# Batch 0's units in four quarter runs, and every second exact addition of weight words on GpSimd

## The chip, the cores and the metric

The kernel runs on one core of one Trainium2 chip. The time is the device time of one execution in microseconds; three runs of the kernel before gave 780.78 to 782.17, with a median of 781.16 us.

## The reference

Attention through packed queries feeds a two-layer network with a rational activation:

```
p_packed = softmax(p k^T / 8) v              # 8 batches, 8 heads, 576 keys, 32 packed rows, 64 wide
x        = softmax(q p_packed^T / 8) p_packed   # 576 queries a batch -> 4608 tokens x 512
h = x @ w_in                                 # 512 -> 2048
P = a0 + a1 h + a2 h^2 + a3 h^3
Q = 1 + |b0| |h| + |b1| h^2
out = (P / (Q + 1e-6)) @ w_out               # 2048 -> 512
```

q, k, v, p, a and the result are float32. The two weight matrices arrive as float64, so the kernel reads them as 64-bit words, 8 MB each, and turns them into float32 on the chip.

## The kernel before

**Tiling.** The tokens of a batch are split into two halves of 288, the 2048 features into eight chunks of 256. A *unit* (batch, half, chunk) is the work on 288 tokens and 256 features; there are 8 x 2 x 8 = 128, walked by u in the order batch, half, chunk. `hidden` (L876) makes h of a unit in PSUM, evaluates the rational function on ScalarE, VectorE and GpSimd (GpSimd adds U and U2; the quotient goes through a logarithm and an exponential on ScalarE), and leaves g in `gh`/`gl`. `acc_block` multiplies g by the rows of w_out and adds up over the eight chunks in two PSUM banks (ring `acc`, 128 tokens each, 256 of the 288); after the last chunk the sum is copied to SBUF and stored. The other 32 tokens of each half gather in `G` and are done for two batches at once in `remainder`.

x itself isn't formed: `m_chunk` multiplies the packed values by a chunk of w_in (tile `win`), so that h is this product (`M`) times the attention's weights (`AH`, `AL`). For batch 0 both are plain float32, for the later ones each operand is split into a high and a low part and three products are taken. The first 12 units (`PLAIN`) also multiply g by w_out undivided, in float32; from unit 12 on w_out is divided into two parts (`divide`, ScalarE and GpSimd), at the steps that `DIVIDE` lists.

**Words.** The weights come in 16 pieces of 1 MB: chunk c of w_in ("in") and of w_out ("out"). `words` sorts them by a due step: "in" c at c - 2, "out" c at c + 3 (`LAG`, as acc_block trails hidden by three units). `load_words` keeps up to five pieces ahead in buffers lent by the rings `m` and `w`; `room` says up to which piece each may be lent. `convert` turns one piece of 128 x 1024 words into float32: two ScalarE operations scale the upper and lower word, then VectorE masks the sign, shifts and joins, and adds the two as integers, exactly (shown in the profile as CUSTOM_DVE_ANT_0 with 2048 columns of 16 bits). The main loop converts one piece a step, and more where a due step asks for it; the first four are converted ahead of the loop.

**Order.** All operations of compute engines and DMAs are only recorded by these functions. `Planner` then sets each engine's order: it works out the data dependences (buffers' turns too), gives each operation a modelled cost, and schedules the list forward by ranks and backward to get new ranks, eight rounds, with 150 ns of slack added to each hand-over between engines on the way back. The best modelled end wins, and the engines' instructions are issued in that order (L288, so nearly all rows of the profile bear this line). In `schedule`, `shares` tells which operations the model keeps from overlapping between VectorE and GpSimd: all of GpSimd's, and of VectorE's the copies, operations with a scalar, and the integer addition, if no operand is in PSUM. Where the plan leaves PE idle in the first 150 us, matmuls with a tile of zeros (L285) are put in; they add nothing to the sums.

The attention of the next batch is spread through the loop's steps as filler (`fill`, `mt` for m_chunk); its first loads and the first words are pinned at the head of SP's queue. Batch 0's attention runs ahead of the first unit.

Of the kernel before, what the change touches and what calls it, by code (L numbers as in the profile page):

```python
# [31 lines left out]
class Planner:  # L32
# [24 lines left out]
    WAY.update({("sync", x): 80 for x in ENGINES})  # L57
    PASS = 200
    FIRST = {"tensor": 700.0, "vector": 800.0, "scalar": 2000.0, "gpsimd": 1400.0, "sync": 700.0}
    ROUNDS = 8  # L60
    SWITCH = 95
    SLACK = 150
    IN_FLIGHT = 8
    DMA_ISSUE, DMA_START, DMA_END = 420, 1400, 1200

# [70 lines left out]
    def shares(self, engine, calls):  # L136

        if engine == "gpsimd":
            return True
        if engine != "vector":  # L140
            return False
        name, args, _ = calls[0]
        aps = [x for x in args if isinstance(x, bass.AP)]
        if any(x.space == PSUM for x in aps):
            return False
        return name in ("tensor_scalar", "tensor_copy") or (name == "tensor_add" and aps[0].dtype == I32)

    def mode(self, engine, calls):

# [38 lines left out]
            edges.append(before)  # L188
        return edges

    def schedule(self, before, after, rank, back=False):

        n = len(rank)
        need = [len(x) for x in before]
        at, start, end = [0.0] * n, [0.0] * n, [0.0] * n
        soon = {e: [] for e in self.ENGINES}
        ready = {e: [] for e in self.ENGINES}
        free = dict.fromkeys(self.ENGINES, 0.0) if back else dict(self.FIRST)
        port = {"vector": 0.0, "gpsimd": 0.0}
        mode, landed, dma = None, [], 0.0  # L200
        for i in range(n):
            if not need[i]:
                heapq.heappush(soon[self.ops[i][0]], (0.0, rank[i], i))
        now = 0.0
        left = n
        while left:
            for e in self.ENGINES:
                while soon[e] and soon[e][0][0] <= now:
                    heapq.heappush(ready[e], heapq.heappop(soon[e])[1:])
                if free[e] > now or not ready[e]:  # L210
                    continue
                if e == "sync" and not back and len(landed) >= self.IN_FLIGHT and landed[-self.IN_FLIGHT] > now:
                    free[e] = landed[-self.IN_FLIGHT]
                    continue
                _, i = heapq.heappop(ready[e])
                left -= 1
                s = now
                if e == "tensor" and not back and self.modes[i] != mode:
                    s += self.SWITCH
                    mode = self.modes[i]  # L220
                if not back and self.shared[i]:
                    s = max(s, port["vector" if e == "gpsimd" else "gpsimd"])
                    port[e] = s + self.costs[i]
                start[i] = s
                end[i] = free[e] = s + self.costs[i]
                if e == "sync":
                    if back:
                        dma = max(dma, end[i]) + self.transfers[i]
                        end[i] = dma + self.DMA_START + self.DMA_END - self.DMA_ISSUE
                    else:  # L230
                        dma = max(dma, s + self.DMA_START) + self.transfers[i]
                        end[i] = dma + self.DMA_END
                        landed.append(end[i])
                for j in after[i]:
                    need[j] -= 1
                    f = self.ops[j][0]
                    way = self.WAY.get((f, e) if back else (e, f), self.PASS)
                    way += self.SLACK * (back and way > 0)
                    at[j] = max(at[j], end[i] + way)
                    if not need[j]:  # L240
                        heapq.heappush(soon[f], (at[j], rank[j], j))
            now = min(
                t
                for e in self.ENGINES
                for t in ([free[e]] if ready[e] else [max(soon[e][0][0], free[e])] if soon[e] else [1e12])
            )
        return start, end

    def order(self):
        n = len(self.ops)  # L250
        self.costs = [self.price(*x) for x in self.ops]
        self.transfers = [self.transfer(calls[0][1]) if engine == "sync" else 0 for engine, calls in self.ops]
        self.shared = [self.shares(*x) for x in self.ops]
        self.modes = [self.mode(*x) for x in self.ops]
        before = self.edges()
        after = [[] for _ in range(n)]
        for i, x in enumerate(before):
            for j in x:
                after[j].append(i)
        rank = list(range(n))  # L260
        best = None
        for r in range(self.ROUNDS):
            start, end = self.schedule(before, after, rank)
            if best is None or max(end) < best[0]:
                best = self.best = max(end), start, end
            s, e = self.schedule(after, before, [-x for x in end], True)
            m = max(e)
            rank = [m - x for x in e]
            rank[: self.pinned] = range(-self.pinned, 0)
        self.end, self.start = best[0], best[1]  # L270
        self.deps, self.t0 = dict(enumerate(before)), best[1]
        return sorted(range(n), key=lambda i: (best[1][i], i))
# [47 lines left out]
def attention_rational_ffn(  # L320
# [106 lines left out]


    words = [(kind, 2 * c, 2) for kind in ("in", "out") for c in range(NCH)]
    due = lambda x: x[1] // 2 + (LAG if x[0] == "out" else -2)  # L430
    words.sort(key=due)
    index = {(kind, i): r for r, (kind, j, n) in enumerate(words) for i in range(j, j + n)}

# [57 lines left out]
    def convert():  # L491
        nonlocal converted
        if converted == len(words):
            return
        load_words(AHEAD)
        (kind, i, n), raw = words[converted], words_in[converted][1]
        x = 4 if kind == "in" else n
        w = raw.bitcast(I32).rearrange("p (x y two) -> p x y two", x=x, two=2)
        lo, hi = w[:, :, :, 0], w[:, :, :, 1]

        if kind == "in":
            dst = win[:, i // 2]
            di = dst.bitcast(I32)
        else:
            dst = undivided(i // 2)
            di = dst.bitcast(I32)
        nc.scalar.activation(hi.bitcast(F32), hi.bitcast(F32), AF.Copy, scale=REBIAS)

        nc.scalar.activation(di, lo.bitcast(U32), AF.Copy, scale=2.0**-29)
        nc.vector.tensor_scalar(lo, hi, -0x80000000, None, ALU.bitwise_and)  # L510
        nc.vector.scalar_tensor_tensor(hi, hi, 3, lo, ALU.logical_shift_left, ALU.bitwise_or)
        nc.vector.tensor_add(dst.bitcast(I32), hi, di)
        converted += 1
        load_words(AHEAD)

# [358 lines left out]
    GS = {}  # L874

    def hidden(bb, x, c):  # L876
        plain = (2 * bb + x) * NCH + c < PLAIN
        mh, ml = (M[bb, c // 2][:, i, :, c % 2 * CF : (c % 2 + 1) * CF] for i in range(2))
        parts = [(mh, AH[bb])] if bb == 0 else [(mh, AH[bb]), (ml, AH[bb]), (mh, AL[bb])]
        U, V, Y = U_ring.next(), V_ring.next()[:, :, 0:HALF], Y_ring.next()  # L880
# [1 line left out]
        for f in range(2):  # L882
            h = h_ring.next()[:, 0:HALF]
            for i, (w, a) in enumerate(parts):
                for g in range(NG):
# [1 line left out]
                        h, w[:, g, f * P : (f + 1) * P], a[:, g, x * HALF : (x + 1) * HALF],  # L887
                        start=g == 0 and i == 0, stop=g == NG - 1 and i == len(parts) - 1,
                    )
            u, y = U[:, f, :], Y[:, f, :]  # L890
            nc.scalar.activation(y, h, AF.Identity, scale=reg_a3, bias=a2)
            nc.scalar.activation(u, h, AF.Abs, scale=reg_b0)
            nc.scalar.activation(U2[:, f, :], h, AF.Square, scale=reg_root)
            nc.vector.tensor_mul(y, y, h)
            nc.vector.scalar_tensor_tensor(y, y, a1, h, ALU.add, ALU.mult)
# [8 lines left out]
        yield  # L904
        r0 = (bb % 2) * REM + x * HREM
        if plain:
            g = GS[bb, x, c] = (gh_ring if c % 2 == 0 else gl_ring).at(c // 2 % 2, dtype=F32)
            for o, cols in ((g, slice(0, HMAIN)), (G[:, 2 * c : 2 * c + 2, r0 : r0 + HREM], slice(HMAIN, HALF))):
                nc.vector.scalar_tensor_tensor(
                    o, V[:, :, cols], 2.0, Y[:, :, cols], ALU.subtract, ALU.mult, reverse0=True  # L910
# [37 lines left out]


    units = [(bb, x, c) for bb in range(B) for x in range(2) for c in range(NCH)]  # L950
    NU = len(units)
    UB = 2 * NCH
    ACC, O = {}, {}

    def acc_block(u, i):
        bb, x, c = units[u]
        if c == 0 and i == 0:
            ACC[bb, x] = [acc_ring.next() for _ in range(2)]
        acc = ACC[bb, x][i]
        cols = slice(i * P, (i + 1) * P)  # L960
        if u < PLAIN:
            for f in range(2):
                g = GS[bb, x, c][:, f, cols]
                nc.tensor.matmul(acc, g, X[c][:, f, :], start=c == 0 and f == 0, stop=c == NCH - 1 and f == 1)
        else:
            gh, gl = GS[bb, x, c]
        for f in range(0 if u < PLAIN else 2):
            accumulate(acc, gh[:, f, cols], gl[:, f, cols], 2 * c + f, c == 0 and f == 0, c == NCH - 1 and f == 1)
        if c < NCH - 1:
            return  # L970
        if i == 0:
            O[bb, x] = o_next()
# [2 lines left out]
        ov = out[bb * T : bb * T + NS * P, :].rearrange(order, i=2, x=2)[:, x]  # L975
        if u == NU - 1 and i == 1:
            nc.vector.tensor_copy(o[:, i, :], acc)
        else:
            nc.scalar.copy(o[:, i, :], acc)
        if u == NU - 1:  # L980
# [20 lines left out]
    STEPS = 16  # L1001
    mt, fill, rem = {}, {}, {}
    for c in range(1, NCH):
        mt[max(0, 2 * c - 3)] = 0, c
    for bb in range(1, B):
        for c in range(0, NCH, 2):
            mt[2 * UB * bb + 2 * c - 7] = bb, c, 2
# [95 lines left out]
```

## Time and profile before

| | |
|---|---|
| median of three runs | 781.16 us (780.78 to 782.17) |
| profiled execution | 780.48 us, span 778.7 us |
| PE / DVE / ACT / POOL busy | 743.9 / 690.6 / 654.8 / 451.8 us |
| mean granted TensorE clock | 0.99 |
| read from and written to HBM | 45.62 MB, 9.44 MB |

Engines: PE is the matmul engine, PEld its weight load, DVE VectorE, ACT ScalarE, POOL GpSimd, SP the queue that issues all DMAs. Times in the views count from the start of the span. A float32 matmul leaves two records. Names such as `w<-w` are output and input tiles with buffer numbers left out; as the words lie in buffers of the rings `m` and `w`, the operations of a conversion show as `m<-m`, `w<-w`, `win<-m,win`, `win<-w,win`, `w<-w,w` or `half<-w,half`.

### The profile page before, as it was taken

The numbers are of one execution on the slowest core, as the hardware profiler recorded it, in microseconds if no ns is written. First come the engines' busy times: TensorE is split into PE (matmuls) and PEld (weight loads), VectorE is DVE, ScalarE is ACT, GpSimd is POOL, SyncE is SP. The second block draws the span as 40 slices with busy tenths as digits, with TensorE's granted clock in tenths as the row PEclk, the third lists the DMA queues.
The fourth block names the chain that finished last, engine by engine and source line by source line (L and its number), as shares of the span: only waits on it lengthen the run. The fifth ranks groups of instructions, "written<-read, shape, count | busy, mean of one in ns | idle before, by whom it ended". The sixth has DMA issues, their size and how long they took to land.

```text
span 778.7 us, 15003 instructions
## 1 busy us (share of the span) xinstructions
PE 743.9 (96%) x5350; PEld 569.8 (73%) x5350; DVE 690.6 (89%) x1295; ACT 654.8 (84%) x1464; POOL 451.8 (58%) x448
## 2 busy tenths in 40 slices
PE   2769999999999999999999999999999999999997
PEld 2435554678788787778788787778778787778886
DVE  4899999987998879998998889998999789998872
ACT  5889978998887988998897898998898798898881
POOL 0012357756695556765596556855586556856663
PEclk9979999999999999999999999999999999999999
DMA  9984260023601155022701128021801023000001
GB/s 299 369 272 145 103 122 28 1 86 53 105 1 55 45 60 98 1 86 38 120 1 55 45 38 120 1 64 41 112 27 55 34 46 40 14 12 17 28 0 42
DMA packets 152028, 56.04 MB, mean 72 GB/s; under 512 B 122256, under 2 KB 141200, under 8 KB 151952
## 3 DMA queue, kind: packets, MB, share of 16 engines
q1 hardware_dynamic: 151952, 55.07, 30.3%
q8 instruction: 42, 0.69, 0.4%
q14 instruction: 34, 0.28, 0.1%
HBM read 45.62 MB, written 9.44 MB: 71 GB/s over the span
## 4 chain that ended last, share of the span: by engine, by line
PE 71%; DVE 12%; ACT 11%; DMA 2%; issue 2%; POOL 1%; SPq 0%; DVEq 0%; ACTq 0%; POOLq 0%
PE acc L288 37%; PE h L288 22%; PE at L288 12%; DVE Y L288 4%; DVE w L288 2%; ACT V L288 2%; ACT Y L288 2%; DVE small L288 2%; DVE kx L288 2%; DMA nat<-in_k_dram 2%; ACT U L288 2%; ACT sq L288 1%; ACT half L288 1%; ACT w L288 1%; DVE V L288 1%
## 5 line engine op out<-in xcount | busy, mean ns | idle before, releaser
L288 POOL TENSOR_TENSOR U<-U,sq 128x576 f32<-128x576 f32 x128 | 184.9, 1444 | 102.1 <-ACT U L288 47.5
L288 PE MATMUL acc<-w,gh 128*128 128x512 f32 x736 | 236.9, 406 | 0.3
L288 PE MATMUL h<-AH,m 128*128 128x288 f32 x1024 | 200.6, 318 | 4.7 <-DVE Y L288 4.0
L288 PEld LDWEIGHTS h<-AH,m 128*128 128x128 f32 x1024 | 160.0, 189 | 45.8 <-DVE Y L288 24.5
L288 POOL TENSOR_TENSOR gl<-Y,gh 128x512 fp32r<-128x512 f32 x116 | 150.4, 1296 | 46.1 <-ACT gh L288 15.2
L288 PEld LDWEIGHTS acc<-w,gh 128*128 128x128 f32 x736 | 133.5, 188 | 44.0 <-issue 9.0
L288 ACT ACTIVATE Y<-h,abS 128x288 f32<-128x288 f32 x256 | 128.5, 518 | 25.0 <-PE h L288 20.1
L288 PE MATMUL acc<-w,gl 128*128 128x512 f32 x384 | 148.1, 412 | 0.2 <-DVE w L288 0.2
L288 ACT ACTIVATE sq<-h 128x288 f32<-128x288 f32 x256 | 108.9, 428 | 34.9 <-PE h L288 26.7
L288 DVE TENSOR_TENSOR Y<-Y,h 128x288 f32<-128x288 f32 x256 | 109.0, 444 | 26.7 <-ACT sq L288 11.6
L288 DVE SCALAR_TENSOR_TENSOR Y<-Y,abS,V 128x576 f32<-128x576 f32 x128 | 102.9, 804 | 27.5 <-ACT V L288 26.7
L288 DVE SCALAR_TENSOR_TENSOR Y<-Y,abS,h 128x288 f32<-128x288 f32 x256 | 124.7, 505 | 2.2
L288 ACT ACTIVATE U<-h 128x288 f32<-128x288 f32 x256 | 102.5, 432 | 11.2 <-DVE V L288 7.4
L288 ACT ACTIVATE V<-U,one 128x576 f32<-128x576 f32 x128 | 99.4, 777 | 10.8 <-DVE Y L288 7.9
L288 PE MATMUL h<-AL,m 128*128 128x288 f32 x448 | 96.0, 295 | 0.0
L288 DVE SCALAR_TENSOR_TENSOR V<-U,V 128x576 f32<-128x576 f32 x128 | 95.8, 749 | 0.0
L288 DVE SCALAR_TENSOR_TENSOR Y<-V,Y 128x576 f32<-128x576 f32 x116 | 86.3, 744 | 1.4
L288 PEld LDWEIGHTS acc<-w,gl 128*128 128x128 f32 x384 | 71.3, 188 | 20.1 <-issue 6.4
L288 ACT ACTIVATE V<-V 128x576 f32<-128x576 f32 x128 | 85.5, 668 | 0.4
L288 PE MATMUL acc<-half,gh 128*128 128x512 f32 x240 | 78.7, 409 | 0.0
L288 ACT CAST gh<-Y 128x512 fp32r<-128x512 f32 x116 | 73.7, 635 | 2.0 <-DVE Y L288 1.3
L288 PEld LDWEIGHTS h<-AL,m 128*128 128x128 f32 x448 | 71.8, 188 | 0.6 <-issue 0.5
(135 smaller groups left out, 955.5 us busy)
## 6 DMA issues: line engine op xcount, KB each, us to landing
w<-in_moe_w_out_dram SPq DMA_DIRECT2D x16, 512.0 KB, 4.4
out_dram<-half SPq DMA_DIRECT2D x15, 512.0 KB, 3.1
nat<-in_k_dram SPq DMA_DIRECT2D x48, 144.0 KB, 3.8
nat<-in_q_dram SPq DMA_DIRECT2D x48, 144.0 KB, 4.3
nat<-in_v_dram SPq DMA_DIRECT2D x24, 256.0 KB, 3.3
m<-in_moe_w_in_dram SPq DMA_DIRECT2D x8, 512.0 KB, 5.7
w<-in_moe_w_in_dram SPq DMA_DIRECT2D x8, 512.0 KB, 9.6
nat<-in_k_dram SPq DMA_DIRECT2D x4, 512.0 KB, 8.5
```

Source lines behind the costliest of these rows:

```text
L288: getattr(getattr(self.nc, engine), name)(*args, **kwargs)
```

## The change

The first 16 units, those of batch 0, run in another order: half 0 with chunks 0 to 3, half 1 with 0 to 3, half 1 with 4 to 7, half 0 with 4 to 7. So a unit's place is no longer its formula but is looked up in `units`; the due steps of words and of m_chunk follow: chunks 4 to 7 of "in" are due at steps 6 to 9 instead of 2 to 5, those of "out" at 11 to 14 instead of 7 to 10. The order of the pieces was in0 to in5, out0, in6, out1, in7, out2, out3, out4 to out7; it becomes in0 to in3, out0, out1, out2, in4, out3, in5, in6, in7, out4 to out7.

Half 0 is now summed in two runs. Its first sum leaves PSUM after chunk 3 (a ScalarE copy into a buffer of the ring AL, which batch 0 doesn't use), and at the end VectorE adds it to the second, where ScalarE copied before.

The exact addition of every second piece (odd in the order of conversion) is issued on GpSimd. The planner's `shares` now counts every VectorE operation with two operands of more than eight columns and none in PSUM, and it tries five values of slack with six rounds each.

```
-    ROUNDS = 8
+    ROUNDS = 6
     SWITCH = 95
-    SLACK = 150
+    SLACK = 60, 100, 150, 220, 300
...
-        return name in ("tensor_scalar", "tensor_copy") or (name == "tensor_add" and aps[0].dtype == I32)
+        wide = sum(self.columns(x) > 8 for x in aps[1:])
+        return wide > 1 or name in ("tensor_scalar", "tensor_copy")
...
-                    way += self.SLACK * (back and way > 0)
+                    way += back * (way > 0)
...
-        rank = list(range(n))
+        first = self.schedule(before, after, list(range(n)))
         best = None
...
+        for slack in self.SLACK:
+            start, end = first
+            for r in range(self.ROUNDS):
+                s, e = self.schedule(after, before, [-x for x in end], slack)
+                m = max(e)
+                rank = [m - x for x in e]
+                rank[: self.pinned] = range(-self.pinned, 0)
+                start, end = self.schedule(before, after, rank)
+                if best is None or max(end) < best[0]:
+                    best = self.best = max(end), start, end
...
-    due = lambda x: x[1] // 2 + (LAG if x[0] == "out" else -2)
+    first = lambda c: c if c < NCH // 2 else c + NCH // 2
+    due = lambda x: first(x[1] // 2) + (LAG if x[0] == "out" else -2)
...
-        nc.vector.tensor_add(dst.bitcast(I32), hi, di)
+        (nc.gpsimd if converted % 2 else nc.vector).tensor_add(dst.bitcast(I32), hi, di)
...
-        plain = (2 * bb + x) * NCH + c < PLAIN
+        u = units.index((bb, x, c))
+        plain = u < PLAIN
...
-            g = GS[bb, x, c] = (gh_ring if c % 2 == 0 else gl_ring).at(c // 2 % 2, dtype=F32)
+            g = GS[bb, x, c] = (gh_ring if u % 2 == 0 else gl_ring).at(u // 2 % 2, dtype=F32)
...
+    cut = NCH // 2
+    units[:2 * NCH] = [(0, x, y * cut + c) for x, y in ((0, 0), (1, 0), (1, 1), (0, 1)) for c in range(cut)]
...
-        if c == 0 and i == 0:
+        fresh, whole = c in ((0, cut) if (bb, x) == (0, 0) else (0,)), c in ((cut - 1, NCH - 1) if (bb, x) == (0, 0) else (NCH - 1,))
+        if fresh and i == 0:
             ACC[bb, x] = [acc_ring.next() for _ in range(2)]
...
+        if not whole:
+            return
         if c < NCH - 1:
+            if i == 0:
+                O[0] = AL_ring.at(0, dtype=F32)
+            nc.scalar.copy(O[0][:, i, 0:DM], acc)
             return
...
+        elif (bb, x) == (0, 0):
+            nc.vector.tensor_add(o[:, i, :], acc, O[0][:, i, 0:DM])
         else:
             nc.scalar.copy(o[:, i, :], acc)
...
-        mt[max(0, 2 * c - 3)] = 0, c
+        mt[max(0, 2 * first(c) - 3)] = 0, c
```

More of the change, by code (lines that the diff above doesn't have):

```diff
@@ L189, in edges, with schedule @@
         return edges
-    def schedule(self, before, after, rank, back=False):
+    def schedule(self, before, after, rank, back=0):
         n = len(rank)
@@ L259, in order @@
                 after[j].append(i)
-        rank = list(range(n))
+        first = self.schedule(before, after, list(range(n)))
         best = None
[L262 to L269, printed above, removed]
+        for slack in self.SLACK:
[8 more added lines that the diff above has]
+                    best = self.best = max(end), start, end
         self.end, self.start = best[0], best[1]
@@ L889, in hidden @@
                     )
-            u, y = U[:, f, :], Y[:, f, :]
+            uf, y = U[:, f, :], Y[:, f, :]
             nc.scalar.activation(y, h, AF.Identity, scale=reg_a3, bias=a2)
-            nc.scalar.activation(u, h, AF.Abs, scale=reg_b0)
+            nc.scalar.activation(uf, h, AF.Abs, scale=reg_b0)
             nc.scalar.activation(U2[:, f, :], h, AF.Square, scale=reg_root)
@@ L963, in acc_block @@
                 g = GS[bb, x, c][:, f, cols]
-                nc.tensor.matmul(acc, g, X[c][:, f, :], start=c == 0 and f == 0, stop=c == NCH - 1 and f == 1)
+                nc.tensor.matmul(acc, g, X[c][:, f, :], start=fresh and f == 0, stop=whole and f == 1)
         else:
@@ L967, in acc_block @@
         for f in range(0 if u < PLAIN else 2):
-            accumulate(acc, gh[:, f, cols], gl[:, f, cols], 2 * c + f, c == 0 and f == 0, c == NCH - 1 and f == 1)
+            accumulate(acc, gh[:, f, cols], gl[:, f, cols], 2 * c + f, fresh and f == 0, whole and f == 1)
+        if not whole:
+            return
         if c < NCH - 1:
+            if i == 0:
+                O[0] = AL_ring.at(0, dtype=F32)
+            nc.scalar.copy(O[0][:, i, 0:DM], acc)
             return
```

## Prediction

> **What bounds the kernel now.** I read the page's first lines, then the busy time by stretches, the chain that ended last, the timeline of the first 140 us, the groups by shape. The page says where time is left.
>
> ```profile
> PE 743.9 (96%) x5350; PEld 569.8 (73%) x5350; DVE 690.6 (89%) x1295; ACT 654.8 (84%) x1464; POOL 451.8 (58%) x448
> PE   2769999999999999999999999999999999999997
> ```
>
> PE is busy nearly everywhere but in the first three of 40 slices (58 us) and the last. The busy time by stretches (columns: PE, PE's weight load, DVE, ACT and POOL, then the granted clock, DMA share and rate) cuts it finer.
>
> ```profile
> 20.00:30.00 10.00, 7.47 (x140) 6.10 (x126) 7.22 (x19) 8.10 (x18) 0.00 (x0) 0.83 1.08 360
> 30.00:46.30 16.30, 9.89 (x101) 4.95 (x99) 16.15 (x39) 12.90 (x24) 0.00 (x0) 0.79 1.05 358
> 46.30:60.00 13.70, 10.89 (x61) 6.00 (x62) 12.83 (x20) 12.92 (x28) 3.11 (x3) 0.87 0.75 245
> 60.00:92.00 32.00, 31.91 (x217) 18.14 (x216) 31.54 (x59) 30.56 (x69) 11.02 (x8) 1.00 0.39 135
> 92.00:139.00 47.00, 46.26 (x279) 24.73 (x280) 46.97 (x90) 39.63 (x81) 29.72 (x22) 1.00 0.31 63
> 110.00:150.00 40.00, 39.26 (x196) 18.87 (x195) 39.10 (x77) 35.50 (x75) 32.97 (x27) 1.00 0.15 29
> ...
> 150.00:303.60 153.60, 153.30 (x1167) 123.89 (x1165) 135.86 (x257) 129.43 (x302) 94.44 (x97) 1.00 0.32 59
> 303.60:481.04 177.44, 176.25 (x1329) 140.57 (x1329) 161.81 (x308) 152.91 (x352) 112.92 (x115) 1.00 0.29 55
> 481.04:658.50 177.46, 175.52 (x1328) 140.57 (x1328) 163.25 (x311) 153.45 (x352) 113.33 (x115) 1.00 0.26 49
> 658.50:778.70 120.20, 115.86 (x640) 94.89 (x640) 95.22 (x171) 92.94 (x210) 75.59 (x76) 0.99 0.06 21
> ```
>
> From 30 to 139 us DVE has no time left (16.15 of 16.30, then 12.83 of 13.70, 31.54 of 32.00, 46.97 of 47.00): 107.5 busy of 109. PE is idle 2.53, 6.41, 2.81, 0.09 and 0.74 us in the five stretches from 20 to 139. From 150 us on PE is the bound: 0.30, 1.19 and 1.94 us idle in the next three.
>
> PE's busy time between 60 and 92 us isn't all work. Line 285 issues matmuls against a tile of zeros where the planner expects PE to wait:
>
> ```profile
> L285 PE MATMUL acc<-half,zero 128*64 128x96 f32 x20 | 2.3, 254 | 0.0
> L285 PE MATMUL acc<-w,zero 128*64 128x96 f32 x18 | 2.1, 254 | 0.0
> ```
>
> These 38 records (columns: busy time, mean ns of one, idle before) are 2.3 + 2.1 = 4.4 us. So PE loses some 8 us between the first hidden matmul and 139 us (2.81 + 4.4 + 0.09 + 0.74), with DVE full beside it, and before that waits on the chain of batch 0's attention, which goes through DVE too. Pieces of that chain (start, length, what):
>
> ```profile
> 27.86 0.10 DVE win L288
> 27.96 0.95 issue
> 28.91 0.34 DVE small L288
> ...
> 39.74 1.08 DVE w L288
> ...
> 44.39 1.14 DVE w L288
> ...
> 46.27 0.82 PE h L288 x2
> ```
>
> Word conversions (the pieces that write win and w) stand in the attention's way: DVE runs whatever comes next in its order, and the attention's small operation of 28.91 us waited for an addition that writes win.
>
> **The change part by part.** The prices, from the groups by shape (first 130 us, then whole run):
>
> ```profile
> L288 DVE SCALAR_TENSOR_TENSOR w<-w 128x1024 int32<-128x1024 int32 x12 | 15.4, 1286 | 0.0
> L288 DVE TENSOR_SCALAR w<-w 128x1024 int32<-128x1024 int32 x12 | 9.0, 753 | 0.0
> L288 DVE CUSTOM_DVE_ANT_0 w<-w,w 128x2048 uint16<-128x2048 uint16 x6 | 7.6, 1262 | 0.0
> ...
> L288 POOL TENSOR_TENSOR U<-U,sq 128x576 f32<-128x576 f32 x128 | 184.9, 1444 | 102.1 <-ACT U L288 47.5
> L288 POOL TENSOR_TENSOR gl<-Y,gh 128x512 fp32r<-128x512 f32 x116 | 150.4, 1296 | 46.1 <-ACT gh L288 15.2
> L288 DVE TENSOR_TENSOR full<-at,full 128x512 f32<-128x512 f32 x12 | 8.2, 686 | 9.0 <-PE at L288 9.0
> L288 ACT COPY half<-acc 128x512 f32<-128x512 f32 x31 | 18.2, 603 | 12.6 <-PE acc L288 6.8 <-PE at L288 5.8
> ```
>
> One conversion on DVE is 0.75 + 1.29 + 1.26 = 3.30 us, the last term the exact addition.
>
> *Additions on GpSimd.* Eight of the 16 conversions lose the 1.26 us on DVE. By the new order of the words these are in1, in3, out1, in4, in5, in7, out5 and out7. The first four conversions begin before 30 us; so two of the eight (in1, in3) lie there, in1's beside idle DVE (worth nothing), in3's at 27.86, in the chain (0.10 + 0.95: 1.05 us). The other six take 6 x 1.26 = 7.6 us out of the full stretch. No integer addition on GpSimd is in this trace. Its nearest rows are float additions of 512 and 576 columns, 1296 and 1444 ns: 148 ns for 64 columns is 2.31 ns a column, and 1024 columns give 1444 + 448 x 2.31 = 2480 ns, my value. Bounds: 1444 ns (as for the shorter row) and twice the value, 4960 ns, if integers or the stride of two words cost as much again. GpSimd is busy 3.11 of 13.70 us and 11.02 of 32.00 us in the stretches up to 92 us. So four of the six lie beside idle GpSimd at no cost to it; out5 and out7 are due at the end, where GpSimd is busy 32.97 of 40 us; 2 x 2.48 fits in the 7.03 left, 2 x 4.96 does not. Behind an addition on GpSimd stand the U additions, for which ACT's logarithm waits.
>
> *What an addition on GpSimd does to DVE.* The timeline shows both engines at once, in one place with operands in SBUF on both sides and in one with an operand of DVE's in PSUM:
>
> ```profile
> 74.78 1.22 DVE L288 CUSTOM_DVE_ANT_0 half<-w,half 128x2048 uint16<-128x2048 uint16 x1
> 75.26 2.01 POOL L288 TENSOR_TENSOR U<-U,sq 128x576 f32<-128x576 f32 x1 [4.74 <-ACT sq L288]
> 76.28 1.56 DVE L288 TENSOR_SCALAR w<-w 128x1024 int32<-128x1024 int32 x1
> ...
> 55.93 1.42 POOL L288 TENSOR_TENSOR U<-U,sq 128x576 f32<-128x576 f32 x1 [5.14 <-ACT sq L288]
> ...
> 56.51 0.75 DVE L288 SCALAR_TENSOR_TENSOR V<-U,V 128x576 f32<-128x576 f32 x1
> ```
>
> In the first, POOL's addition took 2.01 us for 1.42 and DVE's next conversion step 1.56 us for 0.75: they waited for each other. In the second, with V in PSUM, neither is longer. All loop operations of a plain unit on DVE read PSUM, so only conversion steps can be held. I take 0.3 us of DVE a moved addition (between nothing and 0.81, the wait just seen), 6 x 0.3 = 1.8 us; the full addition, 2.48 us, is the upper bound and a rival below. The Trainium skill, SBUF — State Buffer, section "Who interferes with whom", with the section on the two sides ahead of it, has the port pair of the two engines locked for a whole instruction, against DVE operations with two SBUF inputs too. The trace agrees at 75.26 us: 1.42 us after the 1.22 us addition ended at 76.00, at about 77.3 us, POOL is done. This rule speaks against the change, and its worst case is that rival.
>
> *The order of units and words.* Batch 0 now runs chunks 0 to 3 for both halves of the tokens, then 4 to 7. By the due steps, 14 conversions are due by step 8 before and 11 after: 3 x 3.30 = 9.9 us of DVE less ahead of unit 8, which begins here:
>
> ```profile
> 99.51 0.65 PE L288 MATMUL h<-AH,m 128*128 128x288 f32 x2
> ```
>
> They come later, where DVE is also full (46.97 of 47.00), so the order alone removes no DVE work. It moves need from where PE waits (46 to 92 us) to where PE has work queued. The same holds for ACT's two steps a conversion, and for half of the m_chunk copies. The loads of words go the same way: SP issues out0 to out2 ahead of in4; the attention's own loads keep their places, and a word's buffer that GpSimd now releases some 1.2 us later has others of its ring free.
>
> *The sums kept half-way.* The first half's accumulators go to SBUF after chunk 3: two more copies on ACT, 2 x 0.60 us, hidden by ACT's idle (39.63 of 47.00). The end of that half is two DVE additions from PSUM in place of two ACT copies: 2 x 0.69 = 1.4 us more on DVE. The accumulators change hands three times, not two; PE has hidden matmuls in between, so I take 0.2 us, up to 1.2 if it waits for both copies. Plain units stay the first 12, so the matmuls are the same in number and kind.
>
> *The planner.* Five spreads of slack with six rounds each can pick another order for all 128 units. PE's idle in the steady stretches is 0.30, 1.19 and 1.94 us, so it can win 1 to 3 us at most there; I take zero.
>
> *Sum.* DVE's account: -7.6 + 1.8 + 1.4 = -4.4 us of the full stretch, and -1.05 ahead of it: -5.5. PE's account gives what can be used: 1.05 of chain, half of the 2.81 idle (the rest is the latency of the first units), most of the 4.4 of zeros, less 0.2: 1.05 + 1.4 + 3.5 - 0.2 = 5.8 us. Both must hold; I take -5.5. Against the profiled execution, 780.48 us with a span of 778.7, that is 775.0; it lies 0.68 under the median of 781.16, so the forecast is 775.6 us.
>
> **The rivals.** Each is counted from the median, 781.16.
>
> *Given back in the second half:* the conversions moved to units 8 to 12 and the two late additions meet a full DVE and a POOL of 32.97 in 40 us; PE then waits there for in5 to in7 and out4. For it: those two rows. Against: DVE can convert ahead, the words' buffers allow five. Half of the 9.9 us comes back as waiting: 5.5 - 4.9 = 0.6 gained, 780.6.
>
> *The additions hold DVE (the slower side):* place, DVE's conversion steps from 30 to 130 us; price 2.48 us for each of six, 14.9 + 1.4 - 7.6 = +8.7 us, and with the 1.05 of chain gained +7.6, 788.8; it decides from a mean of (7.6 + 1.05 - 1.4) / 6 = 1.2 us of waiting a moved addition. For it: the pair at 75.26. Against: conversion steps are 12 x 3.30 = 39.6 of the 107.5 us, and the rest of DVE's time isn't held. At 1.6 us a wait it is 9.6 + 1.4 - 8.65 = +2.4, 783.5.
>
> *A worse plan for the later batches:* same code from 150 us on in another order; at another 1.94 us in each of the three stretches, -5.5 + 5.8, 781.5. Against: the order before keeps PE at 99% with the same model.
>
> *More than I count:* all of the 2.81 + 4.4 + 0.83 and the 1.05 of chain, with two more of the conversion pieces in the chain (1.08 + 1.14), -11.3: 769.9. Against: DVE's account doesn't pay for it unless less waits on order.
>
> *The change doesn't do what it says:* the integer addition at 4.96 us makes POOL the bound at 110 to 150 us: 2 x 4.96 - 7.03 = 2.9 lost of the 5.5, 778.6.
>
> **How the numbers follow.** Forecast (772 to 778.5) 0.55; given back 0.12; held 0.13; worse plan 0.06; more 0.08; slow integer addition 0.06. The range of eight in ten goes from 769 (the "more" case) to 783, which takes in the cases near zero and leaves out most of "held". A difference under 0.2%, 1.6 us, can't be told from none. Faster: forecast, more, slow addition, and part of given back and worse plan, 0.77. Same: the rest of these two, 0.10. Slower: held, 0.13.
>
> **What would show it.** Right: fewer than ten zero matmuls; the hidden matmul of 46.27 us at 45.3 or before; GpSimd additions of 1024 columns near 2.5 us; DVE's conversion steps at 1.3 and 0.75 us still; PE's idle from 46 to 139 under 2 us; the last unit of batch 0 some 5 us earlier, and the same difference at the end. Wrong: conversion steps on DVE longer by 1 us or more; PE waiting for win or w between 95 and 130 us; idle of more than 2 us in a steady stretch of two batches.

## The result and the profile after

The changed kernel took 776.39 us (median of four, 775.34 to 777.33) against 780.97 us (four runs, 780.40 to 782.17): a ratio of 0.9939 with an interval of 0.9927 to 0.9951, 4.6 us faster. A second measurement, beside the last experiments, gave 776.94 against 782.43 us, 0.9927 (0.9910 to 0.9945).

The profiled execution took 777.33 us, 3.15 less than the one before (780.48). The first lines of the page after, and the busy time by the same stretches as in the prediction:

```profile
PE 738.7 (95%) x5332; PEld 567.8 (73%) x5332; DVE 687.9 (89%) x1289; ACT 653.3 (84%) x1464; POOL 473.0 (61%) x456
PE   1679999999999999999999999999999999999997
```

```profile
20.00:30.00 10.00, 6.60 (x154) 4.75 (x153) 7.98 (x19) 8.36 (x18) 2.42 (x1) 1.00 1.04 345
30.00:46.30 16.30, 11.61 (x106) 6.00 (x105) 15.32 (x37) 11.15 (x22) 1.32 (x2) 0.71 1.04 335
46.30:60.00 13.70, 10.21 (x77) 6.37 (x77) 12.89 (x21) 13.70 (x31) 7.01 (x4) 0.97 1.07 360
60.00:92.00 32.00, 31.34 (x221) 17.59 (x220) 32.00 (x63) 31.98 (x68) 15.02 (x10) 1.00 0.44 144
92.00:139.00 47.00, 46.98 (x264) 23.73 (x263) 45.85 (x83) 39.50 (x83) 35.42 (x24) 1.00 0.21 27
110.00:150.00 40.00, 39.74 (x211) 20.98 (x211) 39.50 (x77) 33.44 (x73) 33.06 (x27) 1.00 0.09 27
```

DVE is still full from 46 to 92 us, and PE is idle 3.49, 0.66 and 0.02 us from 46 to 139 (2.81, 0.09 and 0.74 before). DVE's busy time fell by 2.7 us over the run (690.6 to 687.9), where eight additions of 1.23 us left it and two of 0.69 came. POOL rose by 21 us. The groups by shape say where it went:

```profile
L291 POOL TENSOR_TENSOR w<-w,w 128x1024 int32<-128x1024 int32 x3 | 8.2, 2747 | 2.0 <-DVE w L291 2.0
L291 POOL TENSOR_TENSOR win<-m,win 128x1024 int32<-128x1024 int32 x3 | 7.3, 2417 | 9.9 <-DVE small L291 7.7 <-DVE m L291 2.2
L291 POOL TENSOR_TENSOR win<-w,win 128x1024 int32<-128x1024 int32 x2 | 4.8, 2414 | 6.2 <-DVE w L291 6.2
L291 DVE SCALAR_TENSOR_TENSOR w<-w 128x1024 int32<-128x1024 int32 x11 | 15.0, 1367 | 0.0
L291 DVE TENSOR_SCALAR w<-w 128x1024 int32<-128x1024 int32 x11 | 9.5, 873 | 0.2 <-ACT w L291 0.2
L291 DVE TENSOR_SCALAR m<-m 128x1024 int32<-128x1024 int32 x5 | 4.8, 962 | 9.9 <-ACT win L291 8.4 <-DMA AH<-in_q_dram 1.6
```

A GpSimd addition takes 2.41 us when nothing is in its way. The steps that stayed on VectorE became longer. All of VectorE's rows for the 16 conversions add up to 51.8 us before (masks 11.8, joins 20.3, additions 19.7) and to 46.1 us after (14.3, 21.1, 10.7): 5.7 us less, not 9.0 (what the additions alone fell by, 19.7 to 10.7), because masks and joins grew by 3.3 us, 2.5 of it in the masks. And it isn't conversions alone that wait. The timeline after, in batch 0's attention:

```profile
25.30 2.42 POOL L291 TENSOR_TENSOR win<-m,win 128x1024 int32<-128x1024 int32 x1 [7.74 <-DVE small L291]
...
25.77 1.98 DVE L291 TENSOR_TENSOR small<-small 128x4 f32<-128x4 f32 x1 [0.33 <-ACT small L291]
...
45.27 2.41 POOL L291 TENSOR_TENSOR w<-w,w 128x1024 int32<-128x1024 int32 x1 [2.04 <-DVE w L291]
...
45.74 2.50 DVE L291 TENSOR_SCALAR w<-w 128x1024 int32<-128x1024 int32 x1
```

An operation on four columns, 0.16 us by itself, took 1.98: it ended at 27.75, just behind GpSimd's addition (27.72). The mask of 45.74 us, 0.69 by itself, ended at 48.24, 0.56 behind the end of the addition (47.68). A mask has only one operand in SBUF beside its constant (`lo = hi & 0x80000000`), so it isn't operations with two SBUF operands alone that are held.

### The profile page after: what moved, and what is told of

Read it like the earlier page. It is cut to its first block, busy times and chain, and to the rows that moved or that the text cites. A ratio compares the mean times of both kernels' runs of the same rounds, so it can differ in the third digit from the quotient of the medians.

```text
span 775.5 us, 14985 instructions
## 1 busy us (share of the span) xinstructions
PE 738.7 (95%) x5332; PEld 567.8 (73%) x5332; DVE 687.9 (89%) x1289; ACT 653.3 (84%) x1464; POOL 473.0 (61%) x456
## 4 chain that ended last, share of the span: by engine, by line
PE 68%; DVE 16%; ACT 6%; DMA 5%; issue 2%; POOL 2%; SPq 1%; DVEq 0%; ACTq 0%
PE acc L291 35%; PE h L291 20%; PE at L291 12%; DVE Y L291 7%; DMA m<-in_moe_w_in_dram 2%; DVE V L291 2%; DVE kx L291 2%; DVE m L291 2%; DVE small L291 2%; DMA w<-in_q_dram 1%; ACT Y L291 1%; DMA w<-in_moe_w_in_dram 1%; DMA w<-in_moe_w_out_dram 1%; ACT sq L291 1%; ACT V L291 1%
## 5 line engine op out<-in xcount | busy, mean ns | idle before, releaser
L291 DVE TENSOR_TENSOR Y<-Y,h 128x288 f32<-128x288 f32 x256 | 111.2, 449 | 20.7 <-ACT U L291 7.7
L291 POOL COPY G<-Y 128x64 f32<-128x64 f32 x116 | 27.5, 237 | 76.5 <-DVE Y L291 68.1
```

What stands on the lines that cost most here:

```text
L291: getattr(getattr(self.nc, engine), name)(*args, **kwargs)
```

## The experiments

Each run is timed beside the kernel before on the same chip (782.4 to 782.7 us there).

**The change's three parts, each alone and in pairs.** Parts: the *order* (units, words, the sum kept half-way), the *additions* on GpSimd, the *planner* (five slacks, new sharing rule). With both kernels these are all eight combinations.

Order alone: the changed kernel with the class Planner of before, and with this line as before:

```
-        (nc.gpsimd if converted % 2 else nc.vector).tensor_add(dst.bitcast(I32), hi, di)
+        nc.vector.tensor_add(dst.bitcast(I32), hi, di)
```

> Batch 0's new order (units, words, the sum kept half-way) alone; all exact additions on VectorE and the planner as before. Theory (DVE's account, as in the prediction): the order removes no DVE work and adds two additions of 0.69 us, so with DVE full from 30 to 139 us it gives between +1 and -2 us against the kernel before, 779 to 782. Rival 1 (the order is what pays, because PE waits early and not late): -3 to -5, 776 to 778. Rival 2 (the planner's wider search is what pays): 0.

Additions alone, on the kernel before:

```
-        nc.vector.tensor_add(dst.bitcast(I32), hi, di)
+        (nc.gpsimd if converted % 2 else nc.vector).tensor_add(dst.bitcast(I32), hi, di)
```

> Every second exact addition on GpSimd alone; order of units and words and the planner as before. Theory: -8 x 1.26 us of DVE less some locking, -3 to -5 us, 776 to 778. Rival 1 (the additions hold DVE about as long as they free it; the trace after has 5.8 us less DVE saved than the eight additions are long): between +1 and -1. Rival 2: 0.

Planner alone, the changed class (with its loop over the slacks) in the kernel before:

```
+    SLACK = 60, 100, 150, 220, 300
...
+        wide = sum(self.columns(x) > 8 for x in aps[1:])
+        return wide > 1 or name in ("tensor_scalar", "tensor_copy")
```

> The planner alone (five slacks of six rounds, the new rule of what shares the port); all else as before. Theory: within 1 us of the kernel before, as PE is idle only 3.4 us in the three steady stretches. Rival 2 (the search is what pays): -3 to -5 us, 776 to 778.

Order and planner, the changed kernel with `nc.vector.tensor_add` for all pieces:

> The changed kernel with all exact additions on VectorE again. Theory: loses most of the gain, 779 to 781 (the changed kernel has 776.4). Rival 1 (the additions don't pay, the order does): 775 to 777.5, as the changed kernel or better.

Order and additions, the changed kernel with the class Planner of before:

> The changed kernel with the planner as before (one slack of 150 ns, eight rounds, the old rule of what shares the port). Theory (the additions' locks eat what they free unless the planner knows of them): the conversion steps on VectorE add up to about 50 us, as with the additions alone (50.1), not 46.1 as in the changed kernel, and the time is 0.3 to 0.5% under the kernel before. Rival (the locks don't matter for the time): as the changed kernel, 0.6% under before.

Additions and planner, the kernel before with the additions' line and the class Planner of the changed one:

> GpSimd's additions with the new planner, in the old order of units and words. Theory: the additions' steps on VectorE add up to 46 to 48 us, and the time is 0.2 to 0.4% under before. Rival (the planner's rule does nothing for the additions): 50 us of steps and 0.1 to 0.2% under before, as the additions with the old planner (0.18%).

Measured:

| order | additions | planner | median us | ratio to before (95%) | VectorE's conversion steps, us | granted clock, 20 to 60 us |
|---|---|---|---|---|---|---|
| - | - | - | 782.4 | 1 | 51.8 | 0.83 |
| yes | - | - | 780.59 | 0.9972 (0.9959 to 0.9986) | 51.5 | 0.83 |
| - | yes | - | 780.93 | 0.9982 (0.9968 to 0.9995) | 50.1 | 0.83 |
| - | - | yes | 783.48 | 1.0008 (0.9996 to 1.0021) | 51.0 | 0.79 |
| yes | - | yes | 779.93 | 0.9959 (0.9944 to 0.9975) | 50.7 | 0.87 |
| yes | yes | - | 783.10 | 1.0007 (0.9993 to 1.0020) | 47.1 | 0.84 |
| - | yes | yes | 782.47 | 1.0001 (0.9992 to 1.0010) | 44.4 | 0.79 |
| yes | yes | yes | 776.39 (before 780.97) | 0.9939 (0.9927 to 0.9951) | 46.1 | 0.87 |

(The last two columns are read from one profiled execution each. The rows come from more than one chip; each ratio is against the kernel before on its own.) The parts don't add. The additions change the ratio by -0.18% alone, +0.35% on top of the order, -0.07% on top of the planner and -0.20% on top of both: about nothing on average, and at best 1.6 us (2.5 with the second measurement of the changed kernel) where the working of the prediction had 6.9. The order gives -0.28% alone (2.2 us), -0.49% on the new planner, -0.62% on planner and additions, but +0.25% on the additions with the old planner.

Of the six theories, the planner's held (1.0008 is within its 1 us). The order's stands at its edge: 780.59 us lies in 779 to 782, by the ratio it is 2.2 us where it had at most 2. For order and planner 779.93 lies in 779 to 781, but two thirds of the gain are kept (0.41 of 0.61%), where the theory had most of it lost. The three with additions missed: alone they gave 0.18% and not 3 to 5 us; with the order nothing, and 47.1 us of steps for about 50; with the planner nothing, and 44.4 us for 46 to 48. So the order does most. The additions help alone and on top of both other parts, and cost something on the order with the old planner. Steps alone don't tell the time either: the kernel with the fewest (44.4 us) gains nothing.

Additions alone show the price: eight of them left VectorE, yet its steps fell by 1.7 us only, as masks and joins took 17.5 and 22.0 us (11.8 and 20.3 before); the greater part, from the groups by shape:

```profile
L288 DVE SCALAR_TENSOR_TENSOR w<-w 128x1024 int32<-128x1024 int32 x12 | 17.1, 1427 | 0.1
L288 DVE TENSOR_SCALAR w<-w 128x1024 int32<-128x1024 int32 x12 | 13.5, 1128 | 0.0
```

With order and additions under the old planner the wait reaches PE (timeline):

```profile
77.40 2.42 POOL L288 TENSOR_TENSOR win<-m,win 128x1024 int32<-128x1024 int32 x1
77.76 2.08 DVE L288 SCALAR_TENSOR_TENSOR small<-small 128x2 f32<-128x2 f32 x1
79.76 0.44 DVE L288 TENSOR_TENSOR Y<-Y,h 128x288 f32<-128x288 f32 x1
...
80.75 2.21 PE L288 MATMUL h<-AH,m 128*128 128x288 f32 x8 [1.26 <-DVE Y L288]
```

Two columns of the next batch's attention wait for a GpSimd addition; behind them on VectorE stands the Y of a unit, and for that PE waits 1.26 us.

**Which half of the planner.** The changed kernel with the old rule of what shares the port, five slacks kept:

```
-        wide = sum(self.columns(x) > 8 for x in aps[1:])
-        return wide > 1 or name in ("tensor_scalar", "tensor_copy")
+        return name in ("tensor_scalar", "tensor_copy") or (name == "tensor_add" and aps[0].dtype == I32)
```

> The changed kernel with only the old rule of what shares the port put back, the five slacks kept. Theory: the rule is what keeps additions and conversion steps apart, so the steps on VectorE go back to about 50 us (46.1 in the changed kernel) and 1 to 2 us of the time are lost: 0.35 to 0.5% under before. Rival (the wider search is what pays): 46 us of steps or the time of the changed kernel, 0.6% under before.

778.99 us, 0.9956 (0.9941 to 0.9972). The time is inside the theory's range and 0.17% above the changed kernel, an amount at which the two intervals overlap; the steps are 46.5 us, not 50. So the rule isn't what keeps the steps short, and three quarters of the way from 1.0007 (old planner) to 0.9939 go with the search, as far as one plan of each can tell.

**The additions of batch 0's attention back on VectorE.**

```
-        (nc.gpsimd if converted % 2 else nc.vector).tensor_add(dst.bitcast(I32), hi, di)
+        (nc.gpsimd if converted % 2 and converted >= PRE else nc.vector).tensor_add(dst.bitcast(I32), hi, di)
```

> The changed kernel with the additions of in1 and in3, which fall into batch 0's attention, on VectorE again; six on GpSimd are left. Theory: the small operation of the attention that waited 1.8 us for in3's addition is no longer held, but in3's addition costs 1.2 us on VectorE again; the first hidden matmul comes 0.5 to 1.5 us earlier and the time is 0.6 to 0.8% under before. Rival (the chain of the attention isn't what starts the first units): as the changed kernel within 0.5 us, or 1 us slower.

777.97 us, 0.9935 (0.9922 to 0.9949): as the changed kernel. The mechanism of the theory fell: the small operation isn't held any more, but the first hidden matmul comes later than the changed kernel's 43.42 us, and nothing is lost by it at the end. Its steps come to 48.9 us, 2.8 above the changed kernel's, at the same time. From the timeline:

```profile
26.10 0.16 DVE L291 TENSOR_TENSOR small<-small 128x4 f32<-128x4 f32 x1 [1.85 <-ACT small L291]
...
46.36 3.62 PE L291 MATMUL h<-AH,m 128*128 128x288 f32 x8 [0.25 <-DVE AH L291]
```

**The price of the additions, at nothing and twice.** First the eight moved additions are left out altogether (what that leaves wrong stands in the expectation):

```
-        (nc.gpsimd if converted % 2 else nc.vector).tensor_add(dst.bitcast(I32), hi, di)
+        if converted % 2 == 0:
+            nc.vector.tensor_add(dst.bitcast(I32), hi, di)
```

> The changed kernel with the eight moved additions left out altogether: neither GpSimd nor VectorE adds the lower word's part to every second piece, so these weights are wrong and the time is that of additions that cost nothing. Theory (VectorE's work sets the pace up to 150 us, and the moved additions give back most of what they free through the lock): VectorE's conversion steps add up to 41 to 42 us, and the time falls another 3 to 6 us under the changed kernel, 1.0 to 1.4% under before. Rival (VectorE isn't the bound there, the order and the plan are): within 1.5 us of the changed kernel, 0.4 to 0.8% under before.

774.35 us, 0.9894 (0.9875 to 0.9913). The ratio is in the theory's 1.0 to 1.4%; the steps, 42.8 us, are a little above its 41 to 42, and the 2.6 us under the changed kernel a little below its 3 to 6. Then each is issued twice:

```
+        if converted % 2:
+            nc.gpsimd.tensor_add(lo, hi, di)
         (nc.gpsimd if converted % 2 else nc.vector).tensor_add(dst.bitcast(I32), hi, di)
```

> The changed kernel with each of the eight GpSimd additions issued twice, the first time into the dead lower words. Theory: each further 2.4 us on GpSimd holds VectorE another 0.5 to 1 us, the gain of the changed kernel is gone: 0 to 0.4% over before. Rival (GpSimd's time there is free and the lock doesn't set the time): 0.4 to 0.7% under before.

786.73 us, 1.0062 (1.0041 to 1.0084), more than the theory's 0 to 0.4%. On the same chip the changed kernel has 0.9927, so eight more additions cost 1.35%, 10.5 us (9.8 between the medians), 1.3 us apiece, on an engine that was idle 17 of the 32 us from 60 to 92. The joins on VectorE show it in the groups by shape:

```profile
L291 DVE SCALAR_TENSOR_TENSOR w<-w 128x1024 int32<-128x1024 int32 x11 | 21.9, 1991 | 0.0
L291 DVE SCALAR_TENSOR_TENSOR m<-m 128x1024 int32<-128x1024 int32 x5 | 8.2, 1646 | 0.1
```

They take 1991 ns in the mean (1286 before), and a join that meets nothing takes 1.22 us: the steps come to 55.5 us. With nothing, with one and with two GpSimd additions a piece the ratio goes 0.9894, 0.9927, 1.0062 and the steps 42.8, 46.1, 55.5 us. What PE loses between 46 and 150 us goes with them. The busy time of that stretch, with none, one and two additions a piece (PE's is the number behind 104.00):

```profile
46.00:150.00 104.00, 100.50 (x608) 55.77 (x607) 102.04 (x190) 98.11 (x210) 52.17 (x40) 0.98 0.39 114
46.00:150.00 104.00, 99.60 (x612) 54.48 (x613) 101.95 (x185) 96.48 (x205) 66.41 (x45) 0.99 0.40 115
46.00:150.00 104.00, 96.88 (x604) 55.23 (x603) 100.22 (x168) 86.69 (x184) 72.34 (x40) 0.99 0.37 103
```

PE is idle 3.5, 4.4 and 7.1 us, and 0.9, 2.9 and 8.2 us of its busy time are zeros (6, 20 and 86 records): 4.4, 7.3 and 15.3 us lost. So the rows show that GpSimd's additions hold VectorE, and here the time follows. Two things aren't separated: each of the three has its own plan, and the doubled additions also make GpSimd itself late with the words and with the U additions behind them.

**Shorter pieces.** Each GpSimd addition cut into two of 512 columns:

```
-        (nc.gpsimd if converted % 2 else nc.vector).tensor_add(dst.bitcast(I32), hi, di)
+        if converted % 2:
+            for y in range(2):
+                s = slice(y * x // 2, (y + 1) * x // 2)
+                nc.gpsimd.tensor_add(dst.bitcast(I32)[:, s], hi[:, s], di[:, s])
...
```

> The changed kernel with each GpSimd addition cut into two of 512 columns (about 1.3 us each). Theory: an operation of VectorE that meets one waits at most 1.3 us in place of 2.4; the steps on VectorE add up to 45 us or less and the time is 0.7 to 0.9% under before. Rival (the lock's total is the same, the pieces only add a fixed cost): 46 us or more and 0.5 to 0.65% under before.

779.37 us, 0.9956 (0.9941 to 0.9971), steps 46.7 us: no fewer steps and, if anything, slower than whole additions. The theory fell; of its rival the steps came true (46 us or more), the time not quite (0.44% for 0.5 to 0.65). Its one addition into win from a buffer of the ring w, 1.22 us by itself, took:

```profile
L291 DVE CUSTOM_DVE_ANT_0 win<-w,win 128x2048 uint16<-128x2048 uint16 x1 | 2.3, 2280 | 0.0
```

**The changed kernel again.**

> The changed kernel once more, beside the three others: 0.5 to 0.75% under the kernel before if the first measurement (0.61%) holds.

776.94 us, 0.9927 (0.9910 to 0.9945), as expected. Only the kernel with six of the eight additions on GpSimd (0.9935) is level with it among those that do the whole work.

## Why the prediction was right, and where it was not

The time, 776.39 us, lies in the range and 0.8 us from the forecast of 775.6; faster was given 0.77. That the number came so close is luck: a term that was too large and one that was missed have about cancelled. The working took its whole gain from the additions, 6.9 us, less 1.4 for the two sums at the end; order and planner stood at nothing. Measured, order and planner give two thirds of the gain with no addition moved (0.9959, 3.2 us), and the additions 1.6 to 2.5 us on top.

- *Additions on GpSimd: right in price, wrong in yield.* 2.41 us was measured for the 2.48 worked out from the float rows. The step that failed is "I take 0.3 us of DVE a moved addition" and the sentence ahead of it, "only conversion steps can be held". Masks and joins grew by 3.3 us; beside them three of the attention's operations on two to four columns, with both operands in SBUF, took 1.98, 1.03 and 0.62 us in the profile after, where 0.16 is the length of one by itself. (The one of 1.03 us stands beside a U addition; the kernel without the moved additions has one such too, of 1.00 us.) Between that kernel and the changed one the steps grow by 46.1 - 42.8 = 3.3 us and the small operations by 2.3 us: 0.7 us of VectorE a moved addition. The second eight held the steps alone for 9.4 / 8 = 1.2 us apiece, the point from which the rival "held" was to decide, and the time went over the kernel before. In time the eight additions cost 2.6 us on GpSimd (0.9894 to 0.9927) and 5.1 us on VectorE (0.9894 to 0.9959). So the move is worth 2.5 us with the best plan, 1.6 by the first measurement (0.9939), where the working had 7.6 - 1.8 + 1.05 = 6.9.

  The trace before had shown that small operations are held: this one, beside a U addition, took 1.37 us and ended with it.

```profile
89.51 1.41 POOL L288 TENSOR_TENSOR U<-U,sq 128x576 f32<-128x576 f32 x1 [3.85 <-ACT U L288]
89.56 1.37 DVE L288 TENSOR_TENSOR small<-small 128x4 f32<-128x4 f32 x1
```

  The new rule of the planner leaves out operations of eight columns or fewer, so the plan counts no price for them. And one of the prediction's signs of being wrong, a conversion step on VectorE longer by 1 us or more, did come: the mask of 45.74 us, 2.50 for 0.69.
- *The 1.05 us of chain* didn't come: in3's addition no longer stands on VectorE, but it holds the operation of 25.77 us for 1.8 us. The hidden matmul of 46.27 us is at 45.88, 0.4 earlier and not 1:

```profile
43.42 2.29 PE L291 MATMUL h<-AH,m 128*128 128x288 f32 x4
45.88 1.90 PE L291 MATMUL h<-AH,m 128*128 128x288 f32 x4 [0.17 <-DVE AH L291]
```

- *The order: counted at nothing on DVE, measured at 2.2 us and more in three of four pairs.* The working had said that three conversions fewer would be done ahead of unit 8. In the timeline, VectorE's joins of pieces up to the start of unit 8 are 14 both before (99.5 us) and after (about 98 us): by then the plan has as many pieces converted, whatever the due steps. So the mechanism given (need moved from where PE waits) isn't what the trace shows. Why the order pays isn't settled. The conversions left at the end are later (the last join at 112.2 us after, 110.8 before), and PE has less busy time left from 150 us on (before, then after):

```profile
150.00:778.70 628.70, 620.92 (x4463) 499.92 (x4461) 556.13 (x1044) 528.73 (x1213) 396.28 (x400) 1.00 0.25 48
150.00:780.00 630.00, 616.80 (x4446) 498.65 (x4444) 553.81 (x1042) 527.49 (x1211) 399.72 (x402) 0.99 0.25 47
```

  Before, it was 778.70 - 150 = 628.7 us with 620.92 of PE; after, 625.5 with 616.80. That is 4.1 us less work and 0.9 more idle. Without the zeros both profiles have 5312 matmul records, and 17 more of them are done by 150 us after than before. The sign "the last unit of batch 0 some 5 us earlier, and the same difference at the end" didn't come as written: that unit's hidden matmuls begin 0.7 us earlier (142.99 for 143.70; in the second profile of the changed kernel 144.30), the sums of batch 1's first half leave PSUM 3.7 us earlier (203.88 for 207.55), and the span is 3.2 us shorter. So in this profile the gain is there by 204 us, but not where the working had put it.
- *The planner at zero* was right for it alone (1.0008) and wrong in company: from old to new planner, with order and additions in place, the ratio falls by 0.68%. On the order alone the new planner gives 0.13%, on the additions alone it costs 0.19%. The working looked for its gain in the steady stretches; that it comes from where the additions are placed fits these numbers and isn't shown.
- *POOL as the bound at the end* did not occur: busy 33.06 of 40 us between 110 and 150 (32.97 before), as the plan put seven of the eight additions ahead of 97 us. The last ran from 115.39 us.
- *Zeros:* fewer than ten were forecast, 20 records of 2.9 us are left (38 of 4.4 before). PE's idle time from 46 to 139 us is 4.2 us and not under 2.

```profile
L288 PE MATMUL acc<-w,zero x14: 246/246/297, 65.4 to 103.6; 128*64 128x96 f32 x14
L288 PE MATMUL acc<-half,zero x6: 246/246/297, 117.0 to 117.5; 128*64 128x96 f32 x6
```

- *DVE's account as the limit* was right in kind: the additions at no cost would have given 5.1 us (0.9959 to 0.9894) for 9.8 us of VectorE's work, half a microsecond for each one taken from it.

The rule of the Trainium skill that was weighed, SBUF — State Buffer, section "Who interferes with whom", gives the ports that the two engines share to one instruction for its whole length. The trace agrees where an operation of VectorE with two SBUF inputs met a GpSimd addition, down to two columns: the waits of 2.08 and 1.98 us end within 0.03 us of the addition's own end (79.82 and 27.72 us). The prediction cited it and then priced it from one pair of rows, 0.3 us. For a single operation that meets an addition the rule's length was nearer (1.8 us of waiting); the mean, 0.7 us a moved addition, lies between, as not every addition meets such an operation.

## What to carry to other kernels

Here, work moved from VectorE to GpSimd was paid back in VectorE's time where an operation with its inputs in SBUF met it. Count all such operations of VectorE in the stretch, tiny ones and those with one input and a constant too, and bound the price of the move by the length of the GpSimd operation, not by the idle time of GpSimd. Double the moved work and leave it out once: the two times bracket the price at once, where moving it shows only the difference of two large terms. With an order planned by a model, each edit comes with another plan, so single edits don't add up, and a part's worth is read from several combinations.

## What was not expected

Operations of two or four columns on VectorE were held as long as the large ones: 2.08 us in place of 0.16.

The granted clock of TensorE in the first 60 us moves from kernel to kernel: 0.87 from 46.3 to 60 us before and 0.97 after, 0.79 and 0.71 from 30 to 46.3. Over 20 to 60 us it is 0.83 before and 0.87 after, and that leaves a rival that no run here settles. Of the fourteen profiles (one of each kernel, two of the changed one) the five quickest, 778.4 us and less, all have 0.87 there; the nine others have 0.74 to 0.84, the additions cut in two 0.79 and the doubled ones 0.83. An estimate from PE's 28.25 busy us in that stretch before: at 0.87 in place of 0.83 they would be 1.3 us shorter, a part of the 4.6 us and as much as several differences in the table. Whether the clock makes a plan quicker or only goes with a quick one isn't shown. The additions' price between none and one isn't touched by it, as both profiles have 0.87. The mean clock over the run, 0.99 for both kernels, is too coarse to tell: 0.01 of 778 us is 8 us.

The executions of one kernel spread more than most of these kernels differ: in the experiments the kernel before had 779.51 to 784.94 us in 31 executions. Profiles of one execution each were therefore read for lengths and waits, and the comparisons of time taken from the medians and intervals.
